# Input rows of a chunk moved to another DMA queue, the next chunk's rows ahead of time

## The chip, the cores and the metric

One Trainium2 chip, one core of it. The metric is device time in microseconds (us). The kernel before took 207.96, 210.01 and 210.04 us in three runs, median 210.01. The profiled execution of it spans 208.7 us at a mean granted TensorE clock of 0.992.

The core's engines are named as in the profile: TensorE (PE, with its weight loads PEld), VectorE (DVE), ScalarE (ACT), GpSimd (POOL) and SyncE (SP). SyncE, ScalarE and GpSimd can each issue DMA transfers: SyncE's are queue q1 in the profile, ScalarE's q10, GpSimd's q0.

## The reference

Two layers, one after the other. First a retention recurrence over 768 steps, for 4 batch rows and 8 heads of 64:

```python
gamma = 1.0 - 2.0 ** (-5.0 - np.arange(H))
for t in range(S):
    state = gamma * state + k[:, :, t] (outer) v[:, :, t]
    y[:, :, t] = scale * q[:, :, t] @ state
```

Then, with y reshaped to x of 3,072 tokens by 512, a feed-forward layer with weights of 512 x 2048 and 2048 x 512:

```python
h = x @ w_in
g = 0.5 * h * (1.0 + np.tanh(c * (h + 0.044715 * h * h * h)))
out = g @ w_out
```

Inputs and the output are float32.

## The kernel before

The 768 steps are cut into six chunks of 128. A chunk has four rows (one for each batch), and "row b" below means batch row b of a chunk. For each chunk and row the kernel loads q, k and v (256 KB each, in pieces of 256 bytes), casts them to 16 bits, transposes q and k, forms the scores (`mm_A`, tile a_ps), masks them (`ev_A`, a_sb), adds what comes from the state and from the scores (`mm_yc`, `mm_yi`, tile y_ps), and updates the state st (`mm_s`, `ev_S`, tile s_ps). The result xT of four rows goes through the feed-forward layer: products with w_in into h_ps, gelu into g on ScalarE, and the second product as a scheme of seven block products (Strassen-Winograd) of g, w_out and sums of them (s_g by `g_sums`, t_w by `w_sums`) into o_ps.

The program order on each engine is the order of the source. Attention of the next chunk is laid between pieces ("units") of the feed-forward of this one:

```python
def run(units, after):
    for i, u in enumerate(units):
        u()
        for f, *args in after.get(i, ()):
            f(*args)
```

Loading, casting and transposing:

```python
def ld_tile(nm, c, b):
    if (nm, c, b) not in raw:
        raw[nm, c, b] = ld.tile([128, H, Dh], F32, tag=f"{nm}32", bufs=8 if nm == "v" else 6, name=f"{nm}32")
    return raw[nm, c, b]

def load1(eng, nm, c, b):
    eng.dma_start(
        out=ld_tile(nm, c, b),
        in_=srcs[nm][b, :, c * C:(c + 1) * C, :].rearrange("h p d -> p h d"),
    )

def hold(nm, c, b, until):
    nc.gpsimd.tensor_copy(out=ld_tile(nm, c, b)[0:1, 0, 0:1], in_=until)
...
BANKS = {"h": 2, "o": 2, "att": 4}          # PSUM banks, taken in turn
def mm_T(c, b):                              # transposes on TensorE, into an "att" bank
    ps = bank("att", F16, (128, 2, NHP, 128), "qkT_ps")
    ...                                      # 8 transposes of 128 x 128
def ev_T(c, b, eng=nc.vector):               # copy out of PSUM
    copy_on(eng, qkT_tile(c, b), pss.pop(("T", c, b)))
def dma_T(c, b):                             # the same by DMA, without PSUM
    nc.sync.dma_start_transpose(out=qkT_tile(c, b)..., in_=qk16.pop((c, b))...)
```

Weights come in on GpSimd's queue with a cast from 32 to 16 bits: four parts of w_in, then four of w_out. `hold` writes one element of the tile of q, row 0, chunk 1, from an element of w_out's third part: the load into that tile, and all loads behind it in SyncE's queue, wait until this part has landed.

```python
load_w_in(0)
prep1(PO, "k", 0, 2)
for i in range(1, 4):
    load_w_in(i)
prep1(PO, "k", 0, 3)
prep1(PO, "q", 0, 3)
for i in range(NO):
    load_w_out(i)
...
hold("q", 1, 0, w_out_sb[2][0:1, 0, 0:1])
...
def prep_qk(c, b):
    prep1(AC, "q", c, b)
    prep1(AC, "k", c, b)
    if (c, b) > (1, 2):
        dma_T(c, b)
...
loads(1, "q0", "k0", "q1", "k1", "v0", "q2", "k2", "v1", "q3", "k3")
load_dec()                                   # dec: a table of 256 KB for ev_Y from chunk 1 on
loads(1, "v2", "v3")
...
run(units_0(), {                             # second product of chunk 0, 15 units
    0: [(w_sums, 2), (g_sums, VE, 0, 6, 8)],
    1: [(w_sums, 3)],
    3: [(preps, 1, 0)],
    5: [(att_T, 0)],
    6: [(preps, 1, 1)],
    7: [(att_1A, 0)],
    8: [(att_T, 1), (preps, 1, 2)],
    10: [(att_1A, 1), (preps, 1, 3)],
    11: [(mm_Y, 0, "h"), (att_T, 2, AC), (ev_Y, 1, 0)],
    12: [(mm_Y, 1, "att"), (ev_Y, 1, 1), (mm_s, 1, (0,))],
    13: [(att_1A, 2), (ev_S, 1, (0,))],
    14: [(att_S, 1, 1)],
})
```

After it come the 16 units of chunk 1's first product, eight matmuls of 128 x 256 and one gelu each, which the change touches most (see the diff), then chunk 1's second product in 14 units, in which chunk 2's attention is finished, and then chunks 2 to 5 in a loop that the change leaves alone.

Of the kernel before, what the change touches and what calls it, by code (L numbers as in the profile page):

```python
# [10 lines left out]
F32 = mybir.dt.float32  # L11
# [5 lines left out]
def kernel(  # L17
# [9 lines left out]
    nc = tc.nc  # L27
    B, H, S, Dh = q.shape
# [25 lines left out]
    dec_h = nc.inline_tensor(dec_np.reshape(128, 512).astype(np.float32), name="rr_dec")  # L54
# [3 lines left out]
    ld = ctx.enter_context(tc.tile_pool(name="ld", bufs=2 * B))  # L58
# [13 lines left out]
    dec = const.tile([128, NHP, 128], F32)  # L72

    raw = {}
# [3 lines left out]

    def ld_tile(nm, c, b):
        if (nm, c, b) not in raw:  # L80
            raw[nm, c, b] = ld.tile([128, H, Dh], F32, tag=f"{nm}32", bufs=8 if nm == "v" else 6, name=f"{nm}32")
        return raw[nm, c, b]

    def load1(eng, nm, c, b):
# [5 lines that stand above are left out]
    def load(c):  # L90
        for b in range(B):
            for nm in "qkv":
                load1(nc.sync, nm, c, b)

    def hold(nm, c, b, until):

        nc.gpsimd.tensor_copy(out=ld_tile(nm, c, b)[0:1, 0, 0:1], in_=until)

    nc.sync.dma_start(out=cst[:, :OT + 128], in_=cst_h.ap())
    load1(nc.scalar, "q", 0, 0)  # L100
# [14 lines left out]
        out=misc[:, 0:1], in_=zero[:, 0:1], func=AF.Gelu_apprx_tanh, scale=1.0  # L115
# [8 lines left out]


    st = const.tile([128, B, NHP, 2, 64], F16, name="st")
    nc.gpsimd.memset(st, 0.0)


    mask = const.tile([128, 2, NHP, 128], F32, name="mask")  # L130
    for j in range(2):
        for hp in range(NHP):
            nc.vector.tensor_scalar(
                out=mask[:, j, hp],
# [15 lines left out]
    def prep1(eng, nm, c, b):  # L150
        if nm == "v":
            t = pre.tile([128, H, Dh], F16, tag="v16", bufs=2 * B, name="v16")
        else:
            if (c, b) not in qk16:
                qk16[c, b] = pre.tile([128, 2, H, Dh], F16, tag="qk16", bufs=2 * B, name="qk16")
            t = qk16[c, b][:, "qk".index(nm)]
        src = ld_tile(nm, c, b)
        if (nm == "v") == (c < 1):
            copy_on(eng, t, src)
        else:  # L160
            col = OQ if nm == "q" else OK
            eng.tensor_tensor(  # L162
                out=t,
                in0=src,
                in1=cst[:, col:col + H].unsqueeze(2).broadcast_to([128, H, Dh]),
                op=ALU.mult,
            )
        h16[nm, c, b] = t
# [11 lines left out]
    def bank(tag, dt=F32, shape=(128, NHP, 128), name="ps"):  # L180
        return psum.tile(list(shape), dt, tag=tag, bufs=BANKS[tag], name=name)
# [14 lines left out]
    def ev_T(c, b, eng=nc.vector):  # L196
        copy_on(eng, qkT_tile(c, b), pss.pop(("T", c, b)))

    def dma_T(c, b):

        nc.sync.dma_start_transpose(
            out=qkT_tile(c, b).rearrange("p i hp t -> p (i hp) t"),
            in_=qk16.pop((c, b)).rearrange("p i h d -> p (i h d)"),
        )

    def mm_A(c, b):
        t = qkT[c, b]
        ps = [bank("att", name=f"a_ps{j}") for j in range(2)]
        for hp in range(NHP):
            for j in range(2):  # L210
                nc.tensor.matmul(  # L211
                    out=ps[j][:, hp],
                    lhsT=t[j * 64:(j + 1) * 64, 1, hp],
                    rhs=t[j * 64:(j + 1) * 64, 0, hp],
                    start=True,
                    stop=True,
                )
        pss["A", c, b] = ps

    def ev_A(c, b):  # L220
        ps = pss.pop(("A", c, b))
        for j in range(2):
            s = att.tile([128, NHP, 128], F16, tag=f"a{j}", name=f"a_sb{j}")
            nc.vector.tensor_tensor(out=s, in0=ps[j], in1=mask[:, j], op=ALU.mult)  # L224
            a_sb[c, b, j] = s
# [104 lines left out]
    w_out_sb = [const.tile([128, NF // NO, d_model], F16, name=f"w_out{i}") for i in range(NO)]  # L330
# [9 lines left out]
    def load_w_out(i):  # L340
        n = NF // NO
        nc.gpsimd.dma_start(
            out=w_out_sb[i],
            in_=moe_w_out.rearrange("(fc p) n -> p fc n", p=128)[:, i * n:(i + 1) * n],
        )
# [173 lines left out]
    def units_0():  # L519
# [85 lines left out]
            lambda: (half_p(P4, 1, stop=True), c21()),  # L605
        ]

    def run(units, after):
        for i, u in enumerate(units):
            u()  # L610
            for f, *args in after.get(i, ()):
                f(*args)

    VE, AC, PO, SY = nc.vector, nc.scalar, nc.gpsimd, nc.sync
# [31 lines left out]
    prep1(PO, "q", 0, 3)  # L646
    for i in range(NO):
        load_w_out(i)
    mm_A(0, 1)
    ev_A(0, 1)  # L650
    spin(2)
# [35 lines left out]
        moe1_two(0, fp, *t3)  # L687
    moe1_two(0, 2, half, 2 * half)

    hold("q", 1, 0, w_out_sb[2][0:1, 0, 0:1])  # L690
    for fc in range(6, NF):
        moe1(0, fc)
        if fc == 7:
# [12 lines left out]
    def prep_qk(c, b):  # L706
        prep1(AC, "q", c, b)
        prep1(AC, "k", c, b)
        if (c, b) > (1, 2):
            dma_T(c, b)  # L710

    def preps(c, b):
        prep_qk(c, b)
        prep1(PO, "v", c, b)

    def att_T(b, eng=VE):
        mm_T(1, b)
        ev_T(1, b, eng)

    def loads(c, *what):  # L720
        for nm, b in what:
            load1(SY, nm, c, int(b))

    def load_dec():
        nc.sync.dma_start(out=dec.rearrange("p h t -> p (h t)"), in_=dec_h.ap())

    loads(1, "q0", "k0", "q1", "k1", "v0", "q2", "k2", "v1", "q3", "k3")
    load_dec()
    loads(1, "v2", "v3")

    def att_1A(b):
        mm_A(1, b)
# [2 lines left out]
    def mm_Y(b, tag):  # L735
        mm_yc(1, b, tag)
        mm_yi(1, b)

    run(
        units_0(),  # L740
        {
# [13 lines left out]
    )  # L755


    loads(2, "q0", "k0", "q1", "k1", "q2", "k2", "q3", "k3")
    run(
        [  # L760
            (lambda fp=fp, t=t: moe1_two(1, fp, *t))
            for t in ((0, half), (half, 2 * half))
            for fp in range(NF // 2)
        ],
        {
            1: [(mm_Y, 2, "o"), (ev_Y, 1, 2)],
            2: [(att_1A, 3)],
            3: [(att_S, 1, 2), (g_sums, PO, 1, 0, 4, 0, 1)],
            5: [(mm_Y, 3, "o"), (ev_Y, 1, 3)],
            6: [(att_S, 1, 3), (prep1, AC, "q", 2, 0)],  # L770
            7: [(g_sums, PO, 1, 4, 8, 0, 1), (prep_kT, 2, 0), (loads, 2, "v0", "v1")],
            8: [(prep1, AC, "q", 2, 1)],
            9: [(prep_kT, 2, 1), (loads, 2, "v2", "v3")],
            10: [(prep1, AC, "q", 2, 2)],
            11: [(g_sums, PO, 1, 0, 4, 1, 2), (prep_kT, 2, 2)],
            12: [(prep1, AC, "q", 2, 3)],
            13: [(prep_kT, 2, 3), (load, 3)],
            14: [(att_AY, 1, (), "o", 2, (0, 1), None), (prep1, PO, "v", 2, 0), (prep1, PO, "v", 2, 1)],
            15: [(g_sums, PO, 1, 4, 8, 1, 2), (prep1, PO, "v", 2, 2), (prep1, PO, "v", 2, 3)],
        },  # L780
    )
    run(
        units_w(1),
        {
            4: [(att_AY, 2, (0, 1), "h", 2, (2, 3), AC)],
            6: [(prep_qk, 3, 0)],
            7: [(att_S, 2, 0, 1), (prep_qk, 3, 1)],
            9: [(att_AY, 2, (2, 3), "h", 2, (), AC), (att_S, 2, 2, 3), (prep_qk, 3, 2)],
            10: [(prep1, PO, "v", 3, b) for b in range(B)],
# [56 lines left out]
```

## Time and profile before

| | |
|---|---|
| median of three runs | 210.01 us |
| span of the profiled execution | 208.7 us |
| TensorE busy | 197.5 us (95%) |
| VectorE, ScalarE, GpSimd busy | 102.2, 102.3, 113.1 us |
| TensorE idle from 0 to 10, from 10 to 20 us | 3.95, 1.35 us |
| TensorE idle from 179 to 209 us | 3.8 us |
| loads of rows on SyncE's queue | 66 of 256 KB, 4.3 to 4.4 us from issue to landing |
| DMA transposes | 17, 4.0 us (2.7 to 7.1) |
| parts of w_out | 4 of 512 KB as written, 13.3 us |

How to read it: a busy share is an average over the whole span, so the places where TensorE, the busiest engine, stands still are looked for first, stage by stage, and for each the chain of waits tells what ended it. A row of the timeline, of a group or of the chain begins with start and duration (us), or with the engine and line. `L85` is line 85 of the kernel; the lines of helper functions stand for all their callers, so tiles (qkT, a_ps, h_ps) tell more than lines. In the stages' rows, GB/s counts bytes as written. "Landing" is the time from the issue of a transfer to the point where its data is there.

### The profile page before, as it was taken

The page shows a single profiled execution, that of the slowest core. Times are in us where ns is not written, and L with a number is a line of the kernel's source. Part 1 is how long each engine was busy: PE and PEld are TensorE (multiplying, and loading weights), DVE is VectorE, ACT ScalarE, POOL GpSimd, SP SyncE. Part 2 cuts the span into 40 slices and gives each one's busy share as a digit, 9 for nine tenths or more (in the row PEclk, how much of TensorE's full clock was granted, in tenths as well). Part 3 has the DMA queues.
Part 4 walks back from the last instruction along what each step waited for, and adds up shares of the span by engine and source line. Part 5 has one row for each costly group of instructions (what it writes and reads, how often), then busy time and mean ns, then how long its engine had stood idle before and what let it go on. Part 6 is the DMA issues. An engine that isn't in the chain of part 4 may idle for free.

```text
span 208.7 us, 4545 instructions
## 1 busy us (share of the span) xinstructions
PE 197.5 (95%) x1860; PEld 136.5 (65%) x1860; DVE 102.2 (49%) x237; ACT 102.3 (49%) x180; POOL 113.1 (54%) x113
## 2 busy tenths in 40 slices
PE   5797999999999699999999999999999999999993
PEld 1455746878787488844588744688744788544882
DVE  3356579569960419900449700469601374143420
ACT  2383565454479216566555166445266411466321
POOL 3668000115299995269999159998259990200000
PEclk9999999999999799999999999999999999999999
DMA  7999999997989999999996999841440000400004
GB/s 166 288 256 207 206 207 207 252 246 174 334 198 187 226 234 219 201 215 249 253 241 110 161 316 248 187 101 25 95 184 3 0 0 5 201 0 0 3 22 179
DMA packets 99668, 34.47 MB, mean 165 GB/s; under 512 B 93376, under 2 KB 97856, under 8 KB 99648
## 3 DMA queue, kind: packets, MB, share of 16 engines
q1 hardware_dynamic: 87456, 22.66, 52.1%
q0 software_dynamic: 5664, 9.44, 18.7%
q10 hardware_dynamic: 6528, 2.10, 4.0%
q8 instruction: 14, 0.23, 0.4%
q14 instruction: 6, 0.05, 0.1%
HBM read 27.63 MB, written 6.29 MB: 163 GB/s over the span
## 4 chain that ended last, share of the span: by engine, by line
PE 85%; DMA 8%; ACT 3%; POOL 1%; issue 0%; SPq 0%; POOLq 0%
PE h_ps L352 38%; PE o_ps L460 30%; DMA k<-in_k_dram 6%; PE y_ps L246 3%; PE o_ps L529 3%; PE a_ps L211 3%; PE o_ps L562 3%; DMA qkT<-qk 2%; PE y_ps L233 2%; ACT g L368 2%; POOL qk L162 1%; PE s_ps L270 1%; PE qkT_ps L191 1%; ACT qk L146 1%; ACT s_p L540 0%
## 5 line engine op out<-in xcount | busy, mean ns | idle before, releaser
L352 PE MATMUL h_ps<-xT,w_in 128*128 128x512 f16 (+2 forms) x488 | 88.3, 336 | 0.5 <-ACT g L368 0.5
L368 ACT ACTIVATE g<-h_ps 128x512 f16<-128x512 f32 (+1 forms) x98 | 57.6, 590 | 35.8 <-PE h_ps L352 35.7
L352 PEld LDWEIGHTS <-w_in 128*128 128x128 f16 x488 | 45.8, 98 | 38.0 <-issue 2.2
L224 DVE TENSOR_TENSOR a_sb<-a_ps,mask 128x512 f16<-128x512 f32 x48 | 30.2, 683 | 44.0 <-PE a_ps L211 44.0
L391 POOL TENSOR_TENSOR s_g<-g 128x512 f16<-128x512 f16 x32 | 36.9, 1152 | 10.4 <-ACT g L368 10.4
L460 PEld LDWEIGHTS <-s_g 128*128 128x128 f16 x320 | 30.2, 98 | 4.7 <-POOL s_g L391 0.7
L162 POOL TENSOR_TENSOR v<-v,cst 128x512 f16<-128x512 f32 x20 | 20.4, 1043 | 19.8 <-DMA v<-in_v_dram 19.8
L460 PE MATMUL o_ps<-t_w,s_g 128*128 128x256 f16 x240 | 28.1, 273 | 0.0
L460 PEld LDWEIGHTS <-g 128*128 128x128 f16 x240 | 24.0, 100 | 4.1
L289 DVE SCALAR_TENSOR_TENSOR st<-st,cst,s_ps 64x128 f16<-64x128 f16 (+1 forms) x80 | 20.6, 318 | 0.7 <-PE s_ps L270 0.5
L460 PE MATMUL o_ps<-w_out,g 128*128 128x256 f16 x160 | 19.1, 280 | 0.0
L391 POOL TENSOR_TENSOR s_g<-s_g,g 128x512 f16<-128x512 f16 x16 | 18.4, 1153 | 1.3
L391 POOL TENSOR_TENSOR s_g<-g,s_g 128x512 f16<-128x512 f16 x16 | 18.5, 1155 | 0.0
L262 DVE TENSOR_TENSOR xT<-y_ps,dec 128x512 f16<-128x512 f32 x20 | 13.0, 686 | 3.7 <-PE y_ps L246 3.6
L493 POOL DMA_DIRECT2D out_dram<-o_sb x8 | 5.9, 737 | 16.2 <-DVE o_sb L391 15.3
L146 ACT CAST qk<-q 128x512 f16<-128x512 f32 x20 | 12.4, 622 | 3.1 <-DMA q<-in_q_dram 3.1
L146 ACT CAST qk<-k 128x512 f16<-128x512 f32 x20 | 12.4, 622 | 2.4 <-DMA k<-in_k_dram 2.4
L391 DVE TENSOR_TENSOR o_sb<-o_ps,s_p 128x512 f32<-128x512 f32 (+1 forms) x7 | 4.3, 615 | 18.3 <-issue 9.2
L391 DVE TENSOR_TENSOR s_g<-g 128x512 f16<-128x512 f16 x16 | 6.7, 421 | 11.8 <-ACT g L368 11.8
L483 ACT COPY s_u<-o_ps 128x512 f32<-128x512 f32 (+1 forms) x6 | 3.1, 515 | 17.2 <-PE o_ps L460 12.0
L489 ACT COPY o_sb<-o_ps 128x512 f32<-128x512 f32 (+1 forms) x5 | 2.7, 543 | 17.8 <-PE o_ps L460 17.5
L211 PE MATMUL a_ps<-qkT 64*128 64x128 f16 x192 | 8.6, 224 | 2.0 <-DMA qkT<-qk 1.8
(59 smaller groups left out, 169.5 us busy)
## 6 DMA issues: line engine op xcount, KB each, us to landing
k<-in_k_dram SPq DMA_DIRECT2D x22, 256.0 KB, 4.4
q<-in_q_dram SPq DMA_DIRECT2D x22, 256.0 KB, 4.4
v<-in_v_dram SPq DMA_DIRECT2D x22, 256.0 KB, 4.3
out_dram<-o_sb POOLq DMA_DIRECT2D x10, 512.0 KB, 4.8
w_in<-in_moe_w_in_dram POOLq DMA_DIRECT2D x4, 512.0 KB, 9.7
w_out<-in_moe_w_out_dram POOLq DMA_DIRECT2D x4, 512.0 KB, 13.3
q<-in_q_dram ACTq DMA_DIRECT2D x2, 256.0 KB, 4.0
v<-in_v_dram ACTq DMA_DIRECT2D x2, 256.0 KB, 5.1
```

Source lines behind the costliest of these rows:

```text
L146: eng.copy(out=out, in_=in_)
L162: eng.tensor_tensor(out=t, in0=src, in1=cst[:, col:col + H].unsqueeze(2).broadcast_to([128, H, Dh]), op=ALU.mult,)
L211: nc.tensor.matmul(out=ps[j][:, hp], lhsT=t[j * 64:(j + 1) * 64, 1, hp], rhs=t[j * 64:(j + 1) * 64, 0, hp], start=True, stop=True,)
L224: nc.vector.tensor_tensor(out=s, in0=ps[j], in1=mask[:, j], op=ALU.mult)
L246: nc.tensor.matmul(out=y_ps[j * 64:(j + 1) * 64, hp], lhsT=h16["v", c, b][:, 2 * hp + j], rhs=a_sb[c, b, j][:, hp], start=(c == 0), stop=True,
L262: nc.vector.tensor_tensor(out=x, in0=ps, in1=dec, op=ALU.mult)
L289: nc.vector.scalar_tensor_tensor(out=t[:, :, hp], in0=t[:, :, hp], scalar=cst[sl, OG + hp:OG + hp + 1], in1=s_ps[sl, :, hp], op0=ALU.mult, ...
L352: nc.tensor.matmul(out=out, lhsT=w_in_sb[wi][:, kc, wr * 128:(wr + 1) * 128], rhs=xT[c][:, kc, t0:t1], start=(kc == 0), stop=(kc == NHP - ...
L368: nc.scalar.activation(out=out, in_=in_, func=AF.Gelu_apprx_tanh, scale=1.0)
L391: eng.tensor_tensor(out=out, in0=in0, in1=in1, op=op)
L460: nc.tensor.matmul(out=po, lhsT=lhs(c, lk, fp, a), rhs=rhs(rk, fp), start=(new and fp == 0 and (last or a == 0)), stop=(stop and fp == NP ...
L529: nc.tensor.matmul(out=ps[k][:, a], lhsT=lhs(0, lk, fp, a), rhs=rhs(rk, fp), start=(first and fp == 0 and a == 0), stop=(stop and fp == NP ...
```

## The change

Four things move together.

- **Queues.** Rows of chunk 1 are no longer loaded by SyncE after a hold. GpSimd issues them right behind w_out on its own queue, eight before and four after it has seen w_out's last part. SyncE's queue is held by the table dec instead (one element of it is written from w_out's fourth part) and goes on with dec and all twelve rows of chunk 2.
- **Buffers.** So that q and k of chunk 2 need not wait for those of chunk 1 to be cast, q and k get eight buffers each instead of six, and v six instead of eight.
- **Order.** Casts of chunk 2's q and k on ScalarE begin after unit 4 of chunk 1's first product, not after unit 6, and so do the DMA transposes that follow them; chunk 3's loads are issued at unit 11, not 13.
- **Engines.** Chunk 1's row 3 is transposed on TensorE, as its other rows are, and the zeroing of st goes from GpSimd to VectorE.

It is meant to have the rows of chunks 1 and 2 in flight without a pause when w_out has landed, and chunk 2's transposes done before TensorE asks for them.

```diff
-            raw[nm, c, b] = ld.tile(..., bufs=8 if nm == "v" else 6, name=f"{nm}32")
+            raw[nm, c, b] = ld.tile(..., bufs=6 if nm == "v" else 8, name=f"{nm}32")
...
-    def hold(nm, c, b, until):
-        nc.gpsimd.tensor_copy(out=ld_tile(nm, c, b)[0:1, 0, 0:1], in_=until)
...
-    nc.gpsimd.memset(st, 0.0)
+    nc.vector.memset(st, 0.0)
...
     for i in range(NO):
         load_w_out(i)
+    loads(PO, 1, "q0", "k0", "q1", "k1", "v0", "v1", "q2", "k2")
...
-    hold("q", 1, 0, w_out_sb[2][0:1, 0, 0:1])
+    nc.gpsimd.tensor_copy(out=dec[0:1, 0, 0:1], in_=w_out_sb[3][0:1, 0, 0:1])
+    nc.sync.dma_start(out=dec.rearrange("p h t -> p (h t)"), in_=dec_h.ap())
+    loads(PO, 1, "q3", "k3", "v2", "v3")
+    loads(SY, 2, *[x + str(b) for nm in ("qk", "v") for b in range(B) for x in nm])
...
-        if (c, b) > (1, 2):
+        if c > 1:
             dma_T(c, b)
...
-    loads(1, "q0", "k0", "q1", "k1", "v0", "q2", "k2", "v1", "q3", "k3")
-    load_dec()
-    loads(1, "v2", "v3")
...
-    loads(2, "q0", "k0", "q1", "k1", "q2", "k2", "q3", "k3")
     run(
         [... 16 units of chunk 1's first product ...],
         {
+            0: [(att_T, 3)],
             1: [(mm_Y, 2, "o"), (ev_Y, 1, 2)],
             2: [(att_1A, 3)],
             3: [(att_S, 1, 2), (g_sums, PO, 1, 0, 4, 0, 1)],
-            5: [(mm_Y, 3, "o"), (ev_Y, 1, 3)],
-            6: [(att_S, 1, 3), (prep1, AC, "q", 2, 0)],
-            7: [(g_sums, PO, 1, 4, 8, 0, 1), (prep_kT, 2, 0), (loads, 2, "v0", "v1")],
-            8: [(prep1, AC, "q", 2, 1)],
-            9: [(prep_kT, 2, 1), (loads, 2, "v2", "v3")],
-            10: [(prep1, AC, "q", 2, 2)],
-            11: [(g_sums, PO, 1, 0, 4, 1, 2), (prep_kT, 2, 2)],
-            12: [(prep1, AC, "q", 2, 3)],
-            13: [(prep_kT, 2, 3), (load, 3)],
+            4: [(prep1, AC, "q", 2, 0)],
+            5: [(mm_Y, 3, "o"), (ev_Y, 1, 3), (prep_kT, 2, 0)],
+            6: [(att_S, 1, 3), (prep1, AC, "q", 2, 1)],
+            7: [(g_sums, PO, 1, 4, 8, 0, 1), (prep_kT, 2, 1)],
+            8: [(prep1, AC, "q", 2, 2)],
+            9: [(prep_kT, 2, 2)],
+            10: [(prep1, AC, "q", 2, 3)],
+            11: [(g_sums, PO, 1, 0, 4, 1, 2), (prep_kT, 2, 3), (load, 3)],
             14: [(att_AY, 1, (), "o", 2, (0, 1), None), (prep1, PO, "v", 2, 0), (prep1, PO, "v", 2, 1)],
             15: [(g_sums, PO, 1, 4, 8, 1, 2), (prep1, PO, "v", 2, 2), (prep1, PO, "v", 2, 3)],
```

More of the change, by code (lines that the diff above doesn't have):

```diff
@@ L80, in ld_tile @@
         if (nm, c, b) not in raw:
-            raw[nm, c, b] = ld.tile([128, H, Dh], F32, tag=f"{nm}32", bufs=8 if nm == "v" else 6, name=f"{nm}32")
+            raw[nm, c, b] = ld.tile([128, H, Dh], F32, tag=f"{nm}32", bufs=6 if nm == "v" else 8, name=f"{nm}32")
         return raw[nm, c, b]
@@ L606, in units_0, with loads @@
         ]
+    def loads(eng, c, *what):
+        for nm, b in what:
+            load1(eng, nm, c, int(b))
     def run(units, after):
@@ L718, in att_T @@
         ev_T(1, b, eng)
[L720 to L725, printed above, removed]
-    loads(1, "q0", "k0", "q1", "k1", "v0", "q2", "k2", "v1", "q3", "k3")
-    load_dec()
-    loads(1, "v2", "v3")
     def att_1A(b):
```

## The prediction

> **What bounds the kernel now.** I read the page's busy shares and its 40 slices, then busy time by stage, then the chain of waits around the one weak slice, then the issues of SyncE's queue there.
>
> From the page: the busy line, and the slices of TensorE (PE), of its granted clock and of the DMA engines (a digit is a tenth, a slice 5.2 us).
>
> ```profile
> PE 197.5 (95%) x1860; PEld 136.5 (65%) x1860; DVE 102.2 (49%) x237; ACT 102.3 (49%) x180; POOL 113.1 (54%) x113
> PE   5797999999999699999999999999999999999993
> PEclk9999999999999799999999999999999999999999
> DMA  7999999997989999999996999841440000400004
> ```
>
> TensorE is the bound: 95% busy. Idle lies at the start, in the last slice, and in slice 14 (67.8 to 73 us), where the clock falls too. DMA is full until about 115 us. The stages there (span; busy us of PE, PEld, DVE, ACT, POOL; clock; DMA share; GB/s):
>
> ```profile
> 60.00:65.00 5.00, 5.00 (x45) 4.13 (x43) 1.58 (x8) 4.88 (x11) 4.67 (x6) 1.00 0.84 189
> 65.00:70.00 5.00, 3.24 (x38) 2.27 (x37) 1.29 (x2) 3.45 (x7) 4.92 (x5) 1.00 1.18 202
> 70.00:72.50 2.50, 2.50 (x14) 1.75 (x14) 1.29 (x2) 0.60 (x1) 2.50 (x3) 0.50 1.24 261
> 72.50:75.00 2.50, 2.50 (x21) 2.08 (x20) 0.00 (x0) 0.52 (x1) 2.42 (x4) 0.82 0.88 197
> ```
>
> TensorE stands 1.76 us in the second line, then runs at half clock. The chain of waits there (start us, us, what) says what for:
>
> ```profile
> 63.93 0.50 ACT g L368
> 64.42 0.12 ACT qk L146
> 64.55 5.01 DMA qkT<-qk
> 69.56 0.05 issue
> 69.61 0.40 PE a_ps L211 x8
> 70.00 1.82 PE h_ps L352 x8
> 71.82 5.19 PE o_ps L460 x40
> ```
>
> The scores of chunk 2, row 1 wait for a DMA transpose, issued when ScalarE's cast of k was done, landing 5.01 us later. Its price: 1.76 us of standing, plus the clock: the eight h_ps matmuls take 1.82 us where earlier eights took 0.98 (0.84 lost), and 40 o_ps take 5.19 where 32 at full clock take 3.60, so 4.50 for 40 (0.69 lost). Together **3.3 us**. Elsewhere between 20 us and the last stage the windows show under 0.8 us of idle, so about 4 us (2%) is all that this part of the kernel can give.
>
> **What the Trainium skill says.** "TensorE: Matmul & The Clock Gate", Part 1, has TensorE drop to half clock after an idle window of about 3.4 us, for about as long. The trace agrees on the half clock (0.50), but after 1.76 us of standing. "DMA: Bandwidth & Descriptors", Issuing engines are not separate DMA queues: all queues share the same 16 engines. So the change adds no bandwidth, only order. The same page, Queues, rings and completion order: an engine takes turns between queues packet by packet, and a packet can hold several descriptors. That decides who wins when GpSimd's queue and SyncE's both have work. The trace has one such stretch, 52 to 57 us, when chunk 0's results leave through q0 (GpSimd) beside chunk 2's rows on q1 (SyncE):
>
> ```profile
> DMA packets 2878, 1.69 MB, mean 339 GB/s; under 512 B 2628, under 2 KB 2628, under 8 KB 2877
> ...
> q1 hardware_dynamic: 2597, 0.66, 58.2%
> q0 software_dynamic: 280, 1.02, 53.6%
> ```
>
> Packets of 4 KB on q0 took 60% of the bytes from 256 B packets on q1. How rows of 256 B fare on q0, no part of the trace shows.
>
> **The change part by part.**
>
> 1. Zeroing st goes from GpSimd (1.80 us) to VectorE. VectorE zeroed 256 words in 0.27 us; st is four times that, an estimate of 1.1 us from 1.1 us on. Its next work starts at 2.94 us, when cst lands. Hidden: 0.
>
> 2. Chunk 1 goes behind w_out on GpSimd's queue. The queue's last w_out issue ends at 20.3 us and GpSimd then does nothing until 32.8, so issuing is free (0.74 to 0.92 us each for the loads and stores seen). The first four rows lie in the ring when w_out ends, near 34.4 us (an estimate: the DMA answer for 33.1 to 49 us has 0.17 MB left for q0, 0.8 us at its 205 GB/s, and a little more beside q1). Before, q of row 0 landed at 36.3 us and q of row 2 was cast at 43.85. TensorE idles 0.24 us of 17 from 34 to 51 us, so an earlier arrival buys nothing there. Gain: 0, if nothing comes later.
>
> 3. Chunk 2's rows may start once GpSimd has seen w_out's end (about 36.5 us) instead of from 49.18 us. They were not what ScalarE waited for at 60.08 us, so by itself this is 0 too; it lets part 4 happen.
>
> 4. Casts of chunk 2 start two units sooner (unit 4, not 6), and their transposes stand in SyncE's queue after all of chunk 2's loads rather than between them. Before, row 1's transpose was issued at 64.55 us. ScalarE alternates one g and one cast per unit, 1.0 us, so two units are 2 us. Minus the delay of part 5 (1.4 us), row 1's transpose goes out near 63.1 us and, at the same 5.0 us, lands near 68.1. TensorE wants it at 67.85 + 1.4 = 69.2. **The stall goes: minus 3.3 us.**
>
> 5. Chunk 1's row 3 is transposed on TensorE, in the first unit after 51 us, instead of by DMA. This adds 8 transposes, 0.45 us by the chain's earlier rows. It also needs a PSUM bank of the "att" kind, and going round the four, it is the one that holds the state product of row 0. VectorE empties that one in the first half of this row:
>
> ```profile
> 51.21 3.54 DVE L289 SCALAR_TENSOR_TENSOR st<-st,cst,s_ps 64x64 f16<-64x64 f16 x16
> 54.79 0.69 DVE L262 TENSOR_TENSOR xT<-y_ps,dec 128x512 f16<-128x512 f32 x1
> ```
>
> so at 51.21 + 1.77 = 52.98 us, while TensorE gets there when the first unit ends, 51.13 + 0.92 = 52.05. That is a new wait of 0.9 us. The copy out of PSUM (0.69 us on VectorE) then ends at 54.75 + 0.69 = 55.4, and TensorE, by now late, comes to it at about 55.9: no second wait. **Plus 0.45 + 0.9 = 1.4 us.**
>
> 6. Beside the path: from unit 6 on TensorE ran at ScalarE's pace, about 0.97 us a unit for 0.92 of matmuls. Casts two units sooner fall beside attention matmuls of chunk 1, which gives perhaps 0.2 us back. GpSimd's four groups of sums shift by 1.2 us with the units; the last s_g that TensorE needs first would be there at about 76.2, TensorE comes at 76.4 to 76.8. Narrow, but no wait.
>
> Sum: 210.0 - 3.3 + 1.4 - 0.2 = **207.9 us** if chunk 1 isn't late.
>
> **Rivals.**
>
> *A. The two queues share alike, and chunk 1 comes late.* After about 37.5 us both queues have work. At 228 GB/s in all and half each, a row of 262 KB takes 2.3 us on GpSimd's queue. Three of twelve are through by then; k of row 2 is eighth, so 37.5 + 5 x 2.3 + about 1.3 to land = 50.3 us. TensorE transposes row 2 at 46.9, and the cast must be done: needed by about 45.9. A stall of 4 to 5 us at unit 11, and a half clock after it (1.5 us as above), give 207.9 + 6 = 214. If GpSimd's queue takes nine tenths, k of row 2 is there by 45.5 and nothing happens. For the good case: q0's bytes in the stretch shown, and that four rows have a head start. Against: 256 B pieces on q0 are untried. I give this rival one chance in four, often in a milder form (2 us of stall, 210).
>
> *B. DMA is the bound and the transposes come late anyway.* From 34.4 us to row 1's transpose the engines must move 25 x 0.262 MB of rows and dec, 1.05 MB of results and 0.52 MB of transposes, 8.1 MB. At the rates of before (222 GB/s up to 51 us, 275 up to 60, then 208) that ends at 34.4 + 16.6 + 9 + 9 = 69 us, where it is wanted at 69.2. With both queues full it should be faster (9 to 13 us had 285 to 290 GB/s), so near 63. If not, 1 us of the stall stays and its half clock too: 209.5 to 210. One in six.
>
> *C. Writing descriptors for 256 B pieces is slow on GpSimd.* A w_out issue took 0.76 us, a store 0.74, with fewer pieces each. A row has 1,024. If an issue took 5 us, chunk 1 would be late by 10 us or more. The two values hardly differ between 512 and 256 pieces, so I hold this at one in twenty.
>
> *D. The stall differs from run to run.* One of the three times before is 207.96. A run with the stall mostly gone would be that, and then there is less to win.
>
> **Range and chances.** Good case 207.9 (some six in ten), B around 209.7, A between 210 and 214. The middle of the mixture is 208.4. Low end: all of 3.3 gained, the PSUM wait not there, 206.3. High end: the milder A, 213. Over 2% faster is below 205.8, under my best sum of everything: 0.05. Over 2% slower is above 214.2, only A in full or C: 0.10.
>
> **What would show it.** Right: no wait of a_ps for a DMA transpose near 68 us, clock 1.00 from 65 to 75 us, a wait of qkT_ps for VectorE's st of nearly 1 us near 52 us, chunk 1's casts never holding TensorE. Rival A: TensorE idle between 40 and 56 us, ScalarE or GpSimd waiting for q, k or v of chunk 1, and q1's bytes from 37 to 48 us near q0's. Rival B: the wait for qkT still there, only shorter. C: long issues of rows on GpSimd. The prediction is wrong if chunk 1 lands after 46 us in row 2, or if the clock falls somewhere new.

## The result, and the profile after

The changed kernel took **206.63 us** (median of six runs, 206.54 to 207.56), the kernel before on the same chip 210.01 (six runs, 207.96 to 210.65): a ratio of **0.987**, interval 0.983 to 0.991. That is 1.8 to 3.6 us less. The prediction's middle, 208.4, meant 1.6 less, and its good case, 207.9, 2.1.

From the page of the changed kernel, the busy line and the slices (now 5.1 us each):

```profile
PE 196.4 (96%) x1868; PEld 136.2 (66%) x1868; DVE 103.1 (50%) x239; ACT 102.2 (50%) x180; POOL 121.9 (60%) x124
PE   5798999999999999999999999999999999999993
PEclk9999999999999999999999999999999999999999
DMA  7999999999986899999982999442420000400004
```

The weak slice is gone from TensorE and from its clock. DMA dips in slices 12 to 14 (8, 6, 8; 56 to 72 us), where it had 8, 9, 9 before: the rows are done sooner. The stages show it (span; busy us of PE, PEld, DVE, ACT, POOL; clock; DMA share; GB/s):

```profile
60.00:65.00 5.00, 5.00 (x45) 4.14 (x43) 1.48 (x8) 4.88 (x11) 4.66 (x6) 1.00 0.49 110
65.00:70.00 5.00, 5.00 (x56) 4.00 (x55) 2.22 (x4) 3.12 (x6) 4.92 (x5) 1.00 0.83 132
70.00:72.50 2.50, 2.50 (x26) 2.23 (x24) 0.26 (x1) 0.59 (x1) 2.50 (x3) 1.00 1.21 274
```

TensorE never stands there, and the DMA share from 60 to 65 us fell from 0.84 to 0.49. The chain of waits (start us, us, what) at the place of the old stall:

```profile
59.69 7.72 PE h_ps L348 x64
67.42 0.55 PE a_ps L207 x16
67.97 0.98 PE h_ps L348 x8
68.95 4.37 PE o_ps L456 x40
```

All sixteen scores of rows 0 and 1 run in one go. Eight h_ps take 0.98 us, not 1.82, and 40 o_ps 4.37, not 5.19. With the 1.76 us of standing that is 1.76 + 0.84 + 0.82 = **3.4 us**. Row 1's transpose was issued at 61.84 us and landed at 64.60, in 2.8 us, not 5.0. Chunk 2's twelve rows had all landed by 60.5 us (before: the last v at 71.7). The issue in the timeline of SyncE (start, us):

```profile
61.84 1.23 SPq L197 DMA_TRANSPOSE qkT<-qk  x1
```

The two profiles also differ where nothing was expected to: TensorE's first product of w_in starts at 16.73 us, before at 17.84. So I compare two points on TensorE: S, the start of that first product, and Y, the start of the first y_ps of chunk 2 after the place of the stall. Y minus S is the path that the change touches. Both are read from the timeline of TensorE, where a piece starts up to 0.2 us sooner than in the chain. The later rows come from the experiments below:

| kernel | S | Y | Y - S |
|---|---|---|---|
| before | 17.84 | 76.85 | 59.01 |
| before, profiled again (e9) | 16.60 | 75.73 | 59.13 |
| after | 16.73 | 73.15 | 56.42 |
| after, profiled again (e12) | 16.63 | 73.06 | 56.43 |
| e1, only the casts sooner | 16.71 | 74.14 | 57.43 |
| e2, all but the casts | 16.70 | 73.63 | 56.93 |
| e4, chunk 1's rows on SyncE | 16.96 | 74.37 | 57.41 |
| e6, row 3's copy on ScalarE | 17.90 | 73.76 | 55.86 |
| e10, last loads swapped | 17.20 | 73.62 | 56.42 |
| e11, e6 and e10 together | 16.66 | 72.53 | 55.87 |
| e13, row 3 by DMA on ScalarE | 17.35 | 74.07 | 56.72 |

In each pair that differs only at the start or not at all (before and e9; after, e12 and e10; e6 and e11), Y - S agrees within 0.12 us while S moves by up to 1.24. So the change is worth **2.6 to 2.7 us** on its path; the start is another matter. From Y to the end, the profiles before and after (and e9 and e12) need 131.7 to 132.3 us.

The path falls into four stretches. The last three rows are row 1's transpose in chunk 2, counted from S; its scores are wanted 0.40 us after those of row 0 have begun.

| us | before | after | e1 | e2 | e4 |
|---|---|---|---|---|---|
| S to the scores of chunk 1, row 2 | 31.74 | 31.75 | 32.20 | 31.75 | 32.56 |
| to the scores of chunk 1, row 3 | 4.95 | 5.95 | 4.96 | 5.95 | 5.95 |
| to the first scores of chunk 2 | 12.92 | 12.92 | 12.92 | 12.92 | 12.92 |
| to Y | 9.40 | 5.80 | 7.35 | 6.31 | 5.98 |
| transpose issued | 46.71 | 45.11 | 46.28 | 47.12 | 47.52 |
| transpose landed | 51.72 | 47.87 | 51.80 | 51.30 | 51.78 |
| its scores wanted | 50.01 | 51.02 | 50.48 | 51.02 | 51.83 |

The last stretch, with the stall, is 3.60 us shorter (the 3.4 from above, and 0.2 because two groups of scores in one go take 0.55 us, not twice 0.40). Row 3 on TensorE costs 1.00. Nothing else on the path changed.

### The profile page after: what moved, and what is told of

Same layout as the page of the kernel before. It is cut to its first block, busy times and chain, and to the rows that moved or that the text cites. A ratio compares the mean times of both kernels' runs of the same rounds, so it can differ in the third digit from the quotient of the medians.

```text
span 204.9 us, 4576 instructions
## 1 busy us (share of the span) xinstructions
PE 196.4 (96%) x1868; PEld 136.2 (66%) x1868; DVE 103.1 (50%) x239; ACT 102.2 (50%) x180; POOL 121.9 (60%) x124
## 4 chain that ended last, share of the span: by engine, by line
PE 87%; DMA 7%; DVE 3%; ACT 1%; ACTq 1%; POOL 1%; issue 0%
PE h_ps L348 40%; PE o_ps L456 31%; DMA w_in<-in_moe_w_in_dram 4%; PE o_ps L525 3%; PE y_ps L242 3%; PE a_ps L207 3%; DMA k<-in_k_dram 3%; PE o_ps L558 2%; PE y_ps L229 2%; DVE st L285 2%; PE s_ps L266 1%; PE qkT_ps L187 1%; DVE a_sb L220 1%; ACT g L364 1%; ACTq L85 1%; POOL qk L158 1%
## 5 line engine op out<-in xcount | busy, mean ns | idle before, releaser
L364 ACT ACTIVATE g<-h_ps 128x512 f16<-128x512 f32 (+1 forms) x98 | 57.5, 589 | 33.1 <-PE h_ps L348 32.9
L456 PEld LDWEIGHTS <-g 128*128 128x128 f16 x240 | 23.5, 98 | 3.6
L456 PE MATMUL o_ps<-w_out,g 128*128 128x256 f16 x160 | 18.3, 273 | 0.0
L456 PE MATMUL o_ps<-w_out,s_g 128*128 128x256 f16 x80 | 9.6, 273 | 0.0
```

The costliest lines, as they stand in the source:

```text
L364: nc.scalar.activation(out=out, in_=in_, func=AF.Gelu_apprx_tanh, scale=1.0)
L456: nc.tensor.matmul(out=po, lhsT=lhs(c, lk, fp, a), rhs=rhs(rk, fp), start=(new and fp == 0 and (last or a == 0)), stop=(stop and fp == NP ...
```

## The experiments

**Order or queues (e1, e2).** My theory was step 4: casts two units sooner do it. The rival: rows arrive sooner, so the DMA engines are free when the transposes want them.

e1, the kernel before with nothing but the casts and transposes (and the loads tied to them) two units sooner:

```diff
-            6: [(att_S, 1, 3), (prep1, AC, "q", 2, 0)],
-            7: [(g_sums, ...), (prep_kT, 2, 0), (loads, 2, "v0", "v1")],
+            4: [(prep1, AC, "q", 2, 0)],
+            5: [(mm_Y, 3, "o"), (ev_Y, 1, 3), (prep_kT, 2, 0), (loads, 2, "v0", "v1")],
...          # the other three rows likewise; chunk 3's loads at unit 11, not 13
```

> The kernel before with one part of the change: chunk 2's casts and transposes two units sooner (and chunk 3's loads at unit 11); all queues, buffers and row 3's DMA transpose stay. Theory 'order': in the kernel before, chunk 2's q and k had landed between 52.3 and 63.7 us, early enough for casts from 57 us on, so row 1's transpose is issued near 62.5 us and lands near 67.5 at 5 us; the stall shrinks from 1.76 us to 0.3 or less, the half clock goes, and the time is about 207.0 (3 us less than before). Rival 'queues': the transposes still meet the loads of v on the same queue and land after 68.5 us; at least 1 us of the stall and the half clock stay, 209 to 210.

Measured: 209.42 us (20 runs; before there 210.34), ratio 0.996 (0.994 to 0.999). "Order" falls. The timeline of e1 on TensorE at the two waits (start, us, engine, line, operation, and in brackets the idle time before with what ended it):

```profile
68.56 0.40 PE L211 MATMUL a_ps<-qkT 64*128 64x128 f16 x8 [1.37 <-DMA qkT<-qk]
...
90.16 2.10 PE L352 MATMUL h_ps<-xT,w_in 128*128 128x512 f16 x9 [2.75 <-ACT g L368]
```

Row 1's transpose was issued at 62.99 and landed at 68.51, 5.5 us later, and TensorE still stood 1.37 us. Counted from S it went out only 0.4 us sooner than before, since SyncE was issuing row 0's transpose and two v rows until 62.9, and it landed no sooner at all (51.80, before 51.72). The clock did not halve this time, which "queues" had expected, so the last stretch fell by 2.05 us. Then 2.75 us went again: ScalarE's casts of chunk 3 waited for rows (0.54 to 2.16 us each), and the gelus behind them came late. This profile is of a run of 210.69 us, 1.3 above e1's median, so not every run need have paid that.

e2, the changed kernel with the casts back at units 6 to 13:

```diff
-            4: [(prep1, AC, "q", 2, 0)],
-            5: [(mm_Y, 3, "o"), (ev_Y, 1, 3), (prep_kT, 2, 0)],
+            6: [(att_S, 1, 3), (prep1, AC, "q", 2, 0)],
+            7: [(g_sums, ...), (prep_kT, 2, 0)],
...          # the other three rows likewise
```

> The changed kernel with chunk 2's casts and transposes back at units 6 to 13 (chunk 3's loads at 13); queues, buffers, the row 3 transpose on TensorE and the zeroing on VectorE stay. Theory 'queues': by 61 us all of chunk 2's rows have landed, so row 1's transpose, issued near 64.4 us, runs alone and lands in about 3 us, at 67.5, when TensorE asks for it at 67.5: no stall over 0.3 us, about 206.7, as the changed kernel. Theory 'order': the stall of 1.8 us and its half clock come back, 209.5 to 210.

Measured: 207.43 us, ratio 0.989 (0.986 to 0.992). "Queues" comes nearer, though 206.7 was expected. The wait is still there, but small; from the timeline of TensorE, then of SyncE:

```profile
68.05 0.40 PE L207 MATMUL a_ps<-qkT 64*128 64x128 f16 x8 [0.33 <-DMA qkT<-qk]
```

```profile
63.82 2.84 SPq L197 DMA_TRANSPOSE qkT<-qk  x1
```

So of the path's 2.6 to 2.7 us, 2.1 to 2.2 are there without the sooner casts, and these add 0.5. But the transpose itself landed only 0.4 us sooner than before (51.30 from S): it went out late, and its issue lasted 2.84 us, in the changed kernel 1.23. Of the 1.43 us that TensorE stands less, 0.4 come from that and 1.0 from row 3, which has it ask later; and the clock does not halve. Only both parts together bring the transpose 3.9 us forward, to 47.87.

**What the queue does (e4).** The changed kernel with chunk 1's rows on SyncE's queue again, held on w_out's third part as before; order, buffers and row 3 as in the changed kernel:

```diff
-    loads(PO, 1, "q0", "k0", "q1", "k1", "v0", "v1", "q2", "k2")
...
-    nc.gpsimd.tensor_copy(out=dec[0:1, 0, 0:1], in_=w_out_sb[3][0:1, 0, 0:1])
+    nc.gpsimd.tensor_copy(out=ld_tile("q", 1, 0)[0:1, 0, 0:1], in_=w_out_sb[2][0:1, 0, 0:1])
+    loads(SY, 1, "q0", "k0", "q1", "k1", "v0", "v1", "q2", "k2")
...
-    loads(PO, 1, "q3", "k3", "v2", "v3")
+    loads(SY, 1, "q3", "k3", "v2", "v3")
```

> The changed kernel with chunk 1's rows on SyncE's queue, held until w_out's third part as before, in the changed kernel's order; then dec and chunk 2's rows on the same queue. GpSimd's queue moved a row in 0.76 us (345 GB/s, packets of 4 KB), SyncE's needs about 1.0 us (250 GB/s, packets of 256 B). Theory 'speed of the queue carries the gain': chunk 1 takes 12.5 us instead of 9, chunk 2's rows end near 62 us and push row 1's transpose past 68 us, a stall with its half clock, 208.5 to 209.5. Theory 'room': row 1's transpose is still issued near 62 us and lands near 65 to 66, TensorE asks at 67.4, so nothing waits and the time is 206.6 to 207.2 in spite of the slower rows.

Measured: 208.56 us (207.62 to 210.39), ratio 0.993 (0.990 to 0.996). The DMA view of 33.1 to 49 us, the queue lines as packets, MB, share of 16 engines; first e4:

```profile
DMA packets 13100, 3.69 MB, mean 232 GB/s; under 512 B 12783, under 2 KB 12970, under 8 KB 13098
...
q1 hardware_dynamic: 12895, 3.48, 95.8%
q0 software_dynamic: 203, 0.19, 7.3%
```

and the changed kernel:

```profile
DMA packets 6241, 4.85 MB, mean 305 GB/s; under 512 B 5179, under 2 KB 5343, under 8 KB 6239
...
q0 software_dynamic: 1140, 3.31, 64.9%
q1 hardware_dynamic: 5099, 1.51, 39.3%
```

The same rows of 256 B pieces travel as 12,895 packets of about 270 B on SyncE's queue, but q0's 1,140 packets hold 2.9 KB on average: in the trace its rows go in packets of 4 KB, 64 to a row. Per MB that is 64.9 / 3.31 = 20% of the engines' time in this window, against 95.8 / 3.48 = 28% (packets of two queues overlap, so the shares can add to more than 100%). A row there lands every 0.76 us (36.09, 36.85, 37.61 us and so on, 262 KB each: 345 GB/s); in e4 one lands every 1.1 us from 36.3 to 52.8 us. 1.2 MB more move in the same 16 us.

Neither theory fits e4 as it stood. Its median is in the range of "speed", but in its profile, of its fastest run, the stall was gone: row 1's transpose landed at 68.74, just as it was wanted (68.79). The table tells why. Counted from S the transpose landed at 51.78, as in all four profiles with chunk 1's rows on SyncE (before 51.72, e9 51.83, e1 51.80), whatever the order. TensorE did not wait because it came late itself: 1.00 us by row 3, and 0.81 by chunk 1, for now chunk 1's row 2 was late (in this order v of row 1 goes ahead of it). Its k landed at 44.29 us, not 41.67; ScalarE's casts had waited for their rows, 0.3 to 0.97 us each, and TensorE waited 0.66 us at 46.19 for VectorE behind them. So of the 1.0 us of Y - S that e4 lost against the changed kernel, 0.8 went in chunk 1 and 0.2 at the scores of chunk 2. The median of e4 is 0.9 us above that run; what cost this in its other runs no profile shows.

One rival stays untested: at the kernel's start SyncE's and ScalarE's queues together moved 288 GB/s in packets of 256 B (5 to 11 us). Rows spread over these two were not tried, so what is shown is GpSimd's queue against SyncE's alone.

**The start (e3, e9, e7, e10).** Two theories for the 1.1 us: the zeroing of st, which left GpSimd; or "turn", that row 3's k or v, last in the queues, gets its bytes first by chance. e3 is the changed kernel with the zeroing back:

```diff
-    nc.vector.memset(st, 0.0)
+    nc.gpsimd.memset(st, 0.0)
```

> The changed kernel with st zeroed on GpSimd again. The changed kernel begins chunk 0's products with w_in at 16.73 us, the kernel before at 18.00; in the changed one k of row 3 landed at 13.3 us, ahead of v of row 3, before at 15.2 and after it. Theory 'turn': the order of the last two rows on the queues of SyncE and ScalarE is decided by a few tenths of a us, and the zeroing has nothing to do with it: the start stays near 16.7 us or is either of the two, the time 206.6, or up to 207.8 if the turn falls the other way. Theory 'zeroing': 1.8 us on GpSimd at the start cost it, the start is back at 18.0 us and the time 207.7.

Measured: 206.75 us (before there 210.34), S at 16.88. The zeroing back on GpSimd did not bring the late start back. e9 is the kernel before, unchanged:

> The kernel before, once more, for the start alone. Theory 'turn' (which of row 3's k and v gets its bytes last at the start is settled by when SyncE and ScalarE issue, not by anything in the change): if it is a matter of chance in the kernel before, TensorE's first product of w_in may start here at 16.7 instead of 18.0, and the time is up to 1.1 us lower: 208.0 to 210.3. If it is fixed in the kernel before, the start is at 18.0 again and the time 210.0 to 210.4.

Measured: 209.59 us (207.47 to 211.0), beside 209.36 for the same kernel in the runs around it. Its chain starts as the changed kernel's does:

```profile
16.04 0.62 PE qkT_ps L191 x8
16.66 0.98 PE h_ps L352 x8
...
63.31 5.12 DMA qkT<-qk
68.48 0.40 PE a_ps L211 x8
```

So the kernel before can start early as well, and e6 (below) shows the changed code starting at 17.90. Neither start belongs to one kernel. The stall moves with it (63.31 to 68.48, where the first profile had 64.55 to 69.61), issued 46.71 us after S in both.

In the starts at 17.84 and 17.90, k of row 3 landed at 15.2 to 15.3 us; in all the others by 13.5, and there, but for e13, S comes 0.04 to 0.05 us after w_in's first part has landed. In e10, on ScalarE's queue, k of row 3 goes out ahead of v of row 2.

```diff
-    load1(AC, "v", 0, 2)
+    load1(AC, "k", 0, 3)
...
-    load1(AC, "k", 0, 3)
+    load1(AC, "v", 0, 2)
```

> The changed kernel with the two last loads of chunk 0 on ScalarE's queue swapped: k of row 3 goes out before v of row 2. In the kernel before TensorE's first product of w_in stood at 18.0 us in one profile and at 16.7 in another, in the changed kernel at 16.7 in one and (with row 3's copy on ScalarE) at 18.1 in another: k of row 3 landed at 15.2 or at 13.3. Theory 'turn': k of row 3 decides, since TensorE transposes row 3 ahead of its first product; a place earlier it lands by 12 to 13.5 in every run, the product waits for w_in's first part alone (16.7), and the runs that start late go: median 206.3 to 206.6 beside the changed kernel's 206.6, and no run near 207.5. Rival 'v': v of row 2, now last, is late in its place and holds the first attention of row 2 back by as much: 206.6 to 207.5.

Measured: 206.76 us (206.62 to 207.16), ratio 0.984 (0.981 to 0.987), beside 207.25 for the changed kernel. No run is near 207.5, as "turn" has it, but the median lies above its 206.3 to 206.6. k of row 3 landed at 11.86 (in e12 at 13.19), and still S was 17.20: TensorE waited 0.67 us for w_in's first part, issued at 9.46 us and landed at 17.15 (in e12 9.04 and 16.59). A third kind stands in e13 (below), with S at 17.35: w_in's first part had landed at 16.91, and TensorE waited for nothing from 9 us on, but its clock was at half from 8 to 14 us. From its stages:

```profile
8.00:14.00 6.00, 5.57 (x45) 3.36 (x46) 3.28 (x6) 2.57 (x5) 5.15 (x6) 0.50 1.28 283
```

The changed kernel has 1.00 there. So a late start has at least three forms, "turn" among them; what decides from run to run which one comes is open.

e7 tried the fast queue on chunk 0: its last four tiles on GpSimd's queue.

```diff
-    load1(nc.sync, "q", 0, 3)
-    load1(nc.sync, "v", 0, 3)
+    for nm in ("k", "q", "v"):
+        load1(nc.gpsimd, nm, 0, 3)
+    load1(nc.gpsimd, "v", 0, 2)
...          # and the two loads on ScalarE's queue (v of row 2, k of row 3) taken out
```

> The changed kernel with chunk 0's k, q and v of row 3 and v of row 2 loaded on GpSimd's queue at the very start, instead of last on SyncE's and ScalarE's queues. Theory 'packets' (256 B pieces on GpSimd's queue travel 4 KB at a time, as rows of chunk 1 do at 0.76 us a row, against 1.0 us on SyncE's queue): the last row of chunk 0 lands earlier than its 13.4 to 15.2 us, w_in's first part earlier than 16.7 us, and the whole kernel moves by the same amount: 205.2 to 206.0. Rival 'bytes': the rows of GpSimd's queue take their bytes from row 0 and row 1, on which the first attention waits, and GpSimd's first packet comes 4 us after its issue: the start stays at 16.7 or gets later, 206.6 to 208.

Measured: 210.49 us, ratio 1.005 (1.003 to 1.007). "Bytes" holds, and the loss is larger than its 206.6 to 208. From its chain, then its timeline on TensorE:

```profile
1.85 9.51 DMA k<-in_k_dram
11.42 1.05 POOL qk L159
```

```profile
11.21 0.61 PE L188 MATMUL qkT_ps<-iden,qk 128*128 128x128 f16 x4 [1.87 <-DVE qk L159]
```

The four tiles on q0 landed at 6.73 to 10.89 us, though they are wanted last; k of row 1 came at 11.35 instead of 7.80. TensorE waited for row 1 and then ran the chain of the four rows late: S at 20.37. The DMA view from 8 to 9.5 us shows how the queues share:

```profile
q0 software_dynamic: 133, 0.44, 85.6%
q10 hardware_dynamic: 137, 0.03, 10.7%
q1 hardware_dynamic: 135, 0.03, 10.4%
```

Each queue gets about as many packets as the others, so the one with packets of 4 KB takes nearly all the bytes, whichever it is meant to serve.

**Row 3 on TensorE (e6, e13).** In the changed kernel its scores wait 0.48 us. From the timeline of TensorE, then of VectorE:

```profile
54.43 0.40 PE L207 MATMUL a_ps<-qkT 64*128 64x128 f16 x8 [0.48 <-DVE qkT L144]
```

```profile
50.12 3.53 DVE L285 SCALAR_TENSOR_TENSOR st<-st,cst,s_ps 64x64 f16<-64x64 f16 x16
53.68 0.69 DVE L144 COPY qkT<-qkT_ps 128x1024 f16<-128x1024 f16 x1
```

The copy stands behind 3.5 us of state updates. e6 puts it on ScalarE:

```diff
-            0: [(att_T, 3)],
+            0: [(att_T, 3, AC)],
```

> The changed kernel with row 3's q and k copied out of PSUM on ScalarE, not VectorE. Theory 'copy queue': in the changed kernel the scores of row 3 wait 0.48 us for VectorE's copy, which stands behind 3.5 us of state updates; on ScalarE, where nothing of that length stands, the wait is gone: 206.2 against 206.6 (0.998). Rival 'PE supply': the 0.48 us only moves, because the scores then meet VectorE's later state updates, or ScalarE's gelu and casts of chunk 1 are delayed by the copy's 0.7 us: 206.5 to 207.2.

Measured: 206.21 us (four runs, 205.96 to 207.29), ratio 0.986 (0.980 to 0.993); the profile is of the run of 207.29, a late start. The wait is gone from the trace and Y - S falls by 0.56 to 55.86, in e11 to 55.87: "copy queue" holds. e8, e6 and e7 together:

> The two edits together: row 3's copy on ScalarE, and chunk 0's last rows on GpSimd's queue. If both theories ('copy queue' and 'packets') hold, the gains add, since one lies at 16 us and the other at 54: 204.6 to 205.6. If 'bytes' holds, 206.2 or more.

Measured: 209.64 us, ratio 1.002 (1.000 to 1.005): e7's loss, 0.85 us lower. e13 takes part 5 out and has row 3 transposed by DMA on ScalarE's queue:

```diff
-    def dma_T(c, b):
-        nc.sync.dma_start_transpose(
+    def dma_T(c, b, eng=nc.sync):
+        eng.dma_start_transpose(
...
-        if c > 1:
-            dma_T(c, b)
+        if c > 1 or b > 2:
+            dma_T(c, b, AC if c == 1 else SY)
...
-            0: [(att_T, 3)],
```

> The changed kernel without its fifth part: row 3 of chunk 1 is transposed by a DMA again, as in the kernel before, but on ScalarE's queue, since SyncE now stands at chunk 2's rows. Theory 'sum' (TensorE's path pays 0.45 us for the transposes and 0.48 us for the wait for VectorE's copy): about 0.95 us go, if the transposed row lands by 54.4, where the scores want it: 205.6 to 205.9. Rival 'late': the transpose, issued near 49 us beside chunk 2's rows, takes 5 us or more, as such transposes did under load (5.1 to 5.5), and TensorE waits for it instead: 206.5 to 208.

The measure for it, for e10 and e11 was the changed kernel again:

> The changed kernel once more, as the measure for the other three on the same chip: 206.5 to 206.8, with one run in six or so near 207.6 (a late start).

Measured: e12 207.25 us (206.93 to 207.91), ratio 0.987 (0.983 to 0.991); e13 207.79 (207.52 to 209.28), ratio 0.990 (0.987 to 0.994). In e13 the row landed at 53.51 us, in time, as "sum" needs, but 0.3 us of Y - S were lost, by a third way that neither theory had. From row 2's scores to row 3's it took 4.96 us instead of 5.95, so "sum" was right about its 0.95; but 1.28 were lost ahead of row 2's. The timeline of ScalarE, then of TensorE:

```profile
47.94 1.33 ACTq L197 DMA_TRANSPOSE qkT<-qk  x1
49.32 1.01 ACT L142 COPY qkT<-qkT_ps 128x1024 f16<-128x1024 f16 x1 [2.83 <-PE s_ps L266]
```

```profile
50.38 0.40 PE L207 MATMUL a_ps<-qkT 64*128 64x128 f16 x8 [0.76 <-ACT qkT L142]
```

ScalarE came to the issue at 46.4 and could make it only at 47.94 (the chain puts that down to a row's DMA, 39.23 to 47.87 us). Row 2's copy, behind it on ScalarE, was then late.

**The best of it (e11)**, the swap of e10 and the copy of e6:

> The swap of chunk 0's last loads together with row 3's copy out of PSUM on ScalarE. If 'turn' and 'copy queue' both hold, the first takes the late starts away and the second 0.48 us: 205.9 to 206.2, below the changed kernel in the same runs by 0.4 to 0.7. If either falls: 206.5 or more.

Measured: 206.67 us, ratio 0.984 (0.980 to 0.988), 0.6 below e12 but outside the 205.9 to 206.2. Three of its runs lie at 206.05 to 206.25, with a mean granted clock of 1.000, three at 207.1 to 207.45, with 0.983. Two of e13's eight runs, the profiled one among them, have 0.982 to 0.983 too, so a half clock at the start may be what sets e11's three apart; no profile of them shows it. The shorter path is sure from the traces, but the swap did not take the upper group away. With six runs each the ranges of e11 and e12 overlap, so by times alone it is not shown to be the faster.

## Why the prediction was right or wrong

The time lay in the range, near its low end of 206.3, and the direction was right. The stall went, as said, but the way to it was not the one described. Of the steps:

- **1 (zeroing): right.** It took 0.91 us on VectorE and e3 shows no difference.
- **2 (chunk 1 worth nothing by itself): wrong, and the main miss.** It asked only whether chunk 1 is late for TensorE, and in the profile before it was not (all landed by 49.55 us; after, by 46.98). It was close, though: e1, whose code is the same up to there, lost 0.46 us to it, and e4 0.81. And the step did not ask how long these rows hold up what comes behind them. With nothing changed but the queue and what holds it, the transpose landed 3.9 us sooner from S than in e4 (47.87, 51.78).
- **3 (chunk 2's rows merely permit step 4): wrong in the same way.** They had all landed by 43.8 us from S, in e4 by 48.4, and so row 1's transpose had no rows beside it.
- **4 (the stall goes): right in size, 3.3 said and 3.4 measured, wrong in cause.** With the rows on SyncE, sooner casts left the landing where it was (e1). It kept the old 5.0 us from issue to landing, and 2.8 were measured. Its sum has a slip: 64.55 - 2 + 1.4 is 63.95, not 63.1, so its own figures land at 68.95 for 69.25, with 0.3 us to spare and not 1.1. In the end it was 3.15 us, and that is owed to what steps 2 and 3 left out: with the rows as before (51.8 from S, as in e1 and e4, and wanted at 51.0) some 0.8 us of the stall would have stayed, an estimate from these profiles. So its outcome was partly luck. e2 gives the sooner casts 0.5 us of time.
- **5 (plus 1.4): too high.** The 0.45 of transposes was right. The wait of 0.9 us for a PSUM bank did not come: the transposes followed unit 0 at once (50.92). "No second wait" failed instead: 0.48 us for the copy. Together 0.93; the stretch grew by 1.00.
- **6 (minus 0.2): not there.** From row 3's scores to the first of chunk 2 it is 12.92 us before and after.

On the path the sum should have read -3.6 + 1.0 = -2.6, where I had -2.1: 0.3 too little in step 4 and 0.4 too much in step 5, against 0.2 in step 6 that did not come. The other 0.8 us between the medians (3.4) isn't shown to belong to the change: the start differs by 1.1 us between the two profiles and varies in both kernels.

**Rivals.** A: the share was the right question and the answer went the other way. Where GpSimd's queue and SyncE's both had rows, from 36.5 to 48 us, q0 moved 2.22 MB and q1 1.30, and one of SyncE's issues lasted 5.0 us. "DMA: Bandwidth & Descriptors", Queues, rings and completion order, says that an engine drains a whole packet of one queue before it turns to the next; this agrees, and e7's equal counts of packets (133, 135, 137) with it. But the same page's Issuing engines are not separate DMA queues, from which I took "no bandwidth, only order", is too little here: 305 GB/s against 232 (e4) for rows of the same shape. The measurement decides. B: real; with rows on SyncE it landed at the old moment from S, with 0.05 us to spare in e4 and too late in e1. C: wrong, a row's issue took 0.88 us. D: right that runs differ, but both profiles of before have the stall in full.

## What to carry to other kernels

A transfer that nobody waits for can still be the cause of a wait: ask how long it occupies the DMA engines, and what lies behind it. Before reordering work to get a late transfer out sooner, look at what stands ahead of it in its queue; in this kernel the sooner order alone left the landing where it was. When a wait disappears, see whether the data came sooner or the engine that wanted it later: in e4 it was the latter. And the queue that moved the largest packets also took its bytes first here, so give such a queue what is wanted next, never what is wanted last.

## What the runs showed of the hardware

- Rows of 256 B pieces loaded by GpSimd travelled in packets of 4 KB, a row every 0.76 us (345 GB/s); on SyncE's queue in packets of 256 B, a row every 1.1 us (before and e4). When three queues had packets waiting (e7, 8 to 9.5 us), each got about as many packets, 133 to 137, and so 0.44 MB against 0.03 and 0.03.
- The DMA transpose of row 1 took 2.8 us from issue to landing with no rows beside it, and 5.0 (before), 5.1 (e9) and 5.5 us (e1) with chunk 2's v rows issued around it; in e4, which had the v rows ahead of it, 4.3. Rows are not all of it: in e2 it took 4.2 with none beside it, when SyncE's issue lasted 2.8 us instead of 1.2; the issues before and in e9 and e1 were long as well (2.3 to 2.6). In the changed kernel the long one (2.4) was row 2's, which took 3.7. What makes an issue long is open.
- TensorE's clock halved after 1.76 us (before) and 1.86 us (e9) of standing, not after 1.37 (e1). "TensorE: Matmul & The Clock Gate", Part 1, speaks of an idle window of about 3.4 us. The length of a stand does not decide alone here: near 4 us, at the start, TensorE stood 2.05 to 2.49 us in every profile, and the clock halved soon after in three of them (e9, e10, e13) and not in the others.
